# Shift taps of a long-convolution layer as four 32-row tiles of TensorE in place of two 64-row tiles

## The chip, the cores and the metric

The kernel runs on one core of one Trainium2 chip. The metric is the device time of one execution in microseconds; lower is better. Five engines matter here: TensorE (PE, with its weight loads PEld), VectorE (DVE), ScalarE (ACT), GpSimd (POOL), and SyncE (SP), which issues nearly all transfers to the core's 16 DMA engines.

## The reference

There are two kinds of layer, used in turn: A, B, A, B, on 2048 tokens of 512 channels in bf16. The kernel computes the first pass of A once and reuses its product in the second, because that product depends on `k`, `v` and the filters alone.

```
k_shift = sum over t in 0..3 of k_pad[t : t+2048] * shift_k[:, 3-t]   # causal taps, per channel
kv      = k_shift * v
y       = irfft(rfft(kv, 4096) * rfft(ssm_k, 4096))[:2048] + kv * ssm_D
A(x)    = layernorm(x) * y                                    # q = layernorm(x)
B(x)    = gelu(layernorm(layernorm(x)) @ w1 + b1) @ w2 + b2   # 512 -> 1376 -> 512
x = q;  x += A(layernorm(x));  x += B(...);  x += A(...);  x += B(...)
```

(The second layernorm of a normalized value is part of the reference; what matters for this case is only the part that makes `k_shift * v`.)

## The kernel before, in words

**Two halves.** The first half, to about 100 us, makes the convolution `y` by a Fourier transform that is factored into matmuls. The second half is gating, layernorms and the two matmuls of B, nearly all of it on PE.

**The tiles of the first half.** The 512 channels go in four chunks of 128 (`cc` or `ct`, 0 to 3). The filter (`K`) and the product (`U`) each pass a first stage of matmuls (`S0` to `S3`, L327), are evicted from PSUM (`e`, L334 and L336), are turned (`T0`, `T1`: for `K` by PE at L383, for `U` by transposing DMAs at L456), and pass a second stage with the table `Wt` (`K2..` at L393, `X..` at L486). The spectrum of the filter is also needed with neighbouring partitions exchanged: that is done by copies from SBUF to SBUF, two for each of the pieces `sw00`, `sw01`, `sw11` and `sw10` (L403). Spectra are multiplied on DVE (`T00` to `T33`, L495), go back through PE (`V..`, L504), are evicted (L511, L513), turned by transposing DMAs (`TP..`, L549) and multiplied by a last table (`Y..`, L561 and L570).

**The shift taps.** `k` is brought in turned by four transposing loads (`lk0` to `lk3`, L347): `kT` holds channels on the partitions and tokens along the row. For each chunk, the piece `kv0` to `kv3` (L434) computes the causal taps as matmuls: the weights are 128 tokens of `kT` with a stride of 16, and what streams is a table `DG` of diagonal blocks that holds the tap coefficients. A diagonal block needs only its own rows of the array, so the array is divided into `RT` tiles of `RW = 128 // RT` rows that work side by side, each into its own PSUM bank at a time. With `RT = 2` there are 22 passes of two tiles, with up to 256 columns each. `DG` is made by GpSimd (`dg`, L410) from the coefficients `sT` and from an identity folded to `RW` columns (`IDr`, L293). The two products with `v` are `kvm{cc}1` and `kvm{cc}0` on DVE (L448). They read PSUM and write `uv` in place, and then the first stage `U{cc}S0` and so on can start.

**Memory.** Most data lie in one large SBUF tile, `arena`, at offsets written by hand. Those that matter here: `ZK`, the filter's spectrum, from 0; `KSW`, the target of the swap copies, from 32 KB; `uv` from 64 KB to 80 KB; `kT` from 80 KB. The framework adds semaphore waits where it takes two accesses to `arena` to touch each other.

**The order.** Nothing is scheduled at run time. A string `ORDER` names every piece, with the engine that runs it and the PSUM or buffer slot that it takes. The pieces are recorded in this order and each engine runs its own in order. Around `kv3` and `sw00` it reads:

```
kv3.P01 U1T0.S3 K3T0e.D pb0.G K2S3.P2 kvm31.D K3T1.P3 K2S3e.A sw00.S
kvm30.D K3T1e.A K2T0.P2 U1T1.S pc00.D U3S0.P0 U3S3.P1 K2T0e.D
```

Letters: P is PE, D is DVE, A is ACT, S is SP (a transfer), G is GpSimd. `pa`, `pb` and `pc` are the statistics, scale and application of a layernorm; `lx` loads the rest of the residual.

Of the kernel before, what the change touches and what calls it, by code (L numbers as in the profile page):

```python
# [135 lines left out]
def kernel(ctx: ExitStack, tc: tile.TileContext, A_q, A_k, A_v, A_shift_k, A_ssm_k, A_ssm_D,  # L136
# [17 lines left out]
    KDMA = ()  # L154
    UPE = ()
    TPE = (3,)
    RT = 2
    RW = P // RT

    def apf(t, offset, dims):  # L160
# [64 lines left out]
    def view(t, dims, dtype=None):  # L225
        n = int(np.prod(dims))
        v = t[:, :] if dtype is None else t[:, :].bitcast(dtype)
        names = "abc"[:len(dims)]
        return v[:, 0:n].rearrange("p (%s) -> p %s" % (" ".join(names), " ".join(names)),
                                   **dict(zip(names[1:], dims[1:])))  # L230
# [59 lines left out]
    nc.gpsimd.memset(kT[:, :, 17 - KS:16], 0.0)  # L290
    if RT == 4:
        nc.gpsimd.tensor_tensor(IDh[:], IDt[:, 0:64], IDt[:, 64:P], ALU.add)
    nc.gpsimd.tensor_tensor(IDr[:], *((t[:, RW * i:RW * i + RW] for t in (IDh if RT == 4 else IDt[:, :],) for i in (0, 1))),  # L293
                            ALU.add)
# [118 lines left out]
    for cc in range(4):  # L413
# [3 lines left out]
        def taps(it, cc=cc):  # L417
            tiles = [pf[it["slot"]["ps"]], pf[it["slot"]["ps+"]]]
            seen = set()
            for tau in [0] + list(range(1 - KS, 0)) + list(range(1, NT)):  # L420
                for r in range(RT):
                    rows = slice(RW * r, RW * r + RW)
                    first, end = max(tau, 0), min(tau + KS, NT)
                    while first < end:
                        if RT == 2:
                            last = min(end, first // 8 * 8 + 8)
# [12 lines left out]
        for h in range(2):  # L439
            def mul(it, pe=pe, cc=cc, h=h):  # L440
                c0 = cc * CW + 64 * h
                t = pf[pe["slot"]["ps+" if h else "ps"]]
                if RT == 2:
                    us, k = uv[:, :, c0:c0 + 64], view(t, [NT, 64])
# [279 lines left out]
```

## Time and profile before

| | us |
|---|---|
| median of 3 runs | 260.72 (260.39 to 260.88) |
| the profiled execution: time / span of its trace | 260.88 / 259.2 |
| PE busy in the span | 236.0 (91%) |
| PE weight loads | 144.2 (56%) |
| DVE busy | 172.0 (66%) |
| ACT busy | 145.5 (56%) |
| DMA issued by SP (q1), share of 16 engines | 54.2% |

The span is what the trace covers; the time also has what lies around it. In the page's table of 40 slices each digit stands for about 6.5 us of the span and gives the busy share in tenths. In a list of instructions in order of time, the first number is the start in us from the span's start, the second the duration, and a bracket at the end gives the idle time of that engine just before, and what ended it. SPq is the SP queue: its durations are those of issuing a transfer, not of the transfer. A share of busy DMA engines can be over 1, since transfers that overlap on an engine are added.

### The profile page before, as it was taken

Reading aid. Unit: us, or ns where it says so; the run is one execution under the profiler, and the core shown is the slowest. Engines: PE = TensorE matmul, PEld = TensorE weight load, DVE = VectorE, ACT = ScalarE, POOL = GpSimd, SP = SyncE. Lnnn points to the kernel's source line nnn. Section 1 sums busy time; section 2 is a strip of 40 time slices with the busy share of each in tenths; the row PEclk is TensorE's granted clock in tenths of the full one; section 3 lists DMA queues with packets and bytes.
Section 4 is the critical chain, followed back from the end, with each engine's and each line's share of the span. In section 5 each row is a group of like instructions: output and inputs, shape, how many; then the busy total and the mean of one; then the engine's idle time right before and its main releaser. Section 6 shows DMA issues by size and latency. Waiting matters only on the chain.

```text
span 259.2 us, 4520 instructions
## 1 busy us (share of the span) xinstructions
PE 236.0 (91%) x1800; PEld 144.2 (56%) x1800; DVE 172.0 (66%) x347; ACT 145.5 (56%) x199; POOL 28.3 (11%) x54
## 2 busy tenths in 40 slices
PE   7399999969976668999999999999999999999994
PEld 6378888858976535954444444444444444444441
DVE  0558999998898999989987457567677900120232
ACT  2235798788988827895829238268234285055000
POOL 4210000100000321132201101101101100000000
PEclk9979999999999959999999999999999999999999
DMA  6999999999999999920322120050040140010111
GB/s 251 165 280 271 189 340 271 207 282 310 245 303 179 166 226 344 178 42 0 72 40 53 30 52 4 0 82 0 3 81 0 60 104 0 0 72 9 43 70 52
DMA packets 61961, 32.87 MB, mean 127 GB/s; under 512 B 56722, under 2 KB 58868, under 8 KB 60788
## 3 DMA queue, kind: packets, MB, share of 16 engines
q1 hardware_dynamic: 61186, 32.51, 54.2%
q8 instruction: 14, 0.23, 0.4%
q10 hardware_dynamic: 674, 0.07, 0.3%
q0 software_dynamic: 80, 0.00, 0.2%
q14 instruction: 7, 0.06, 0.1%
HBM read 12.40 MB, written 2.10 MB: 56 GB/s over the span
## 4 chain that ended last, share of the span: by engine, by line
PE 69%; DMA 12%; DVE 8%; ACT 6%; issue 2%; SPq 1%; POOL 0%; ACTq 0%; DVEq 0%; POOLq 0%
PE p_89 L680 10%; PE p_92 L680 8%; PE p_91 L658 8%; PE p_92 L658 8%; PE p_89 L658 7%; PE p_90 L658 7%; PE p_90 L680 6%; PE p_91 L680 5%; DMA arena<-in_A_k_dram 4%; DMA ZT_78<-ZT_76 3%; DMA arena<-arena 2%; ACT arena L315 2%; DMA ZT_82<-ZT_81 2%; DVE arena L317 2%; DVE arena L448 2%
## 5 line engine op out<-in xcount | busy, mean ns | idle before, releaser
L658 PEld LDWEIGHTS <-arena 128*128 128x128 bf16 (+1 forms) x396 | 39.6, 100 | 37.9 <-issue 1.3
L680 PEld LDWEIGHTS <-arena 128*128 128x128 bf16 (+1 forms) x352 | 34.4, 98 | 41.7
L680 PE MATMUL p_89<-arena 128*128 128x512 bf16 (+1 forms) x121 | 27.1, 379 | 0.0
L669 ACT ACTIVATE arena<-p_91,B_71 128x512 bf16<-128x512 f32 (+3 forms) x26 | 15.8, 663 | 18.5 <-PE p_92 L680 9.8
L688 DVE TENSOR_TENSOR arena<-p_89,arena 128x1024 bf16<-128x1024 f32 (+1 forms) x4 | 4.4, 1092 | 31.5 <-PE p_89 L680 31.5
L658 PE MATMUL p_91<-arena 128*128 128x512 bf16 (+3 forms) x104 | 23.3, 367 | 0.0
L658 PE MATMUL p_92<-arena 128*128 128x512 bf16 (+3 forms) x108 | 22.4, 351 | 0.0
L680 PE MATMUL p_92<-arena 128*128 128x512 bf16 (+1 forms) x99 | 22.2, 379 | 0.0
L669 ACT ACTIVATE arena<-p_92,B_71 128x512 bf16<-128x512 f32 (+3 forms) x27 | 15.5, 632 | 11.8 <-PE p_92 L658 11.7
L658 PE MATMUL p_89<-arena 128*128 128x512 bf16 (+1 forms) x96 | 18.9, 343 | 1.2 <-ACT arena L315 1.2
L669 ACT ACTIVATE arena<-p_89,B_71 128x512 bf16<-128x512 f32 (+1 forms) x24 | 13.2, 613 | 12.0 <-PE p_90 L680 7.8
L658 PE MATMUL p_90<-arena 128*128 128x512 bf16 (+2 forms) x88 | 19.2, 360 | 0.0
L680 PE MATMUL p_90<-arena 128*128 128x512 bf16 (+1 forms) x77 | 17.3, 379 | 0.0
L327 PEld LDWEIGHTS <-arena 128*128 128x128 bf16 x128 | 11.9, 97 | 6.4 <-issue 2.0
L669 ACT ACTIVATE arena<-p_90,B_71 128x512 bf16<-128x512 f32 (+2 forms) x22 | 13.1, 645 | 4.0 <-PE p_90 L658 2.3
L578 DVE TENSOR_TENSOR arena<-arena 128x1024 bf16<-128x1024 bf16 (+2 forms) x17 | 11.2, 656 | 1.9 <-ACT arena L315 1.1
L680 PE MATMUL p_91<-arena 128*128 128x512 bf16 (+1 forms) x55 | 12.4, 379 | 0.0
L688 DVE TENSOR_TENSOR arena<-p_92,arena 128x1024 bf16<-128x1024 f32 (+1 forms) x4 | 4.4, 1091 | 11.8 <-PE p_92 L680 11.8
L315 ACT ACTIVATE arena<-p_92 128x2048 bf16<-128x2048 bf16 (+2 forms) x6 | 7.0, 1166 | 8.6 <-PE p_92 L383 6.1
L434 PEld LDWEIGHTS <-arena 64*128 64x128 bf16 x176 | 8.9, 149 | 3.6 <-DMA arena<-in_A_k_dram 2.9
L257 DVE BATCH_NORM_STATS2 lst_105<-arena 128x6 f32<-128x512 bf16 x16 | 10.3, 684 | 0.6 <-DMA arena<-in_A_q_dram 0.5
L257 DVE BATCH_NORM_STATS2 lst_97<-arena 128x6 f32<-128x512 bf16 x16 | 10.2, 682 | 0.0
(193 smaller groups left out, 420.8 us busy)
## 6 DMA issues: line engine op xcount, KB each, us to landing
arena<-arena SPq DMA_DIRECT2D x8, 512.0 KB, 4.8
arena<-in_A_ssm_k_dram SPq DMA_DIRECT2D x4, 512.0 KB, 5.6
arena<-in_A_v_dram SPq DMA_DIRECT2D x2, 1024.0 KB, 7.3
arena<-tabM SPq DMA_DIRECT2D x1, 2048.0 KB, 13.1
arena<-in_A_q_dram SPq DMA_DIRECT2D x1, 1536.0 KB, 7.6
arena<-in_B_w_dram SPq DMA_DIRECT2D x1, 1376.0 KB, 6.6
arena<-in_B_w_dram SPq DMA_DIRECT2D x1, 1280.0 KB, 9.9
Wt<-tabW SPq DMA_DIRECT2D x1, 1024.0 KB
```

The costliest lines, as they stand in the source:

```text
L257: nc.vector.bn_stats(self.st[:, i, h, :], xg(g, i, i + 1, c0, c9)[:, 0, :])
L315: nc.scalar.activation(d, s, AF.Copy)
L317: nc.vector.tensor_copy(d, s)
L327: nc.tensor.matmul(o[:, i, :], src[:, 4 * q + i, cs], Ft[:], start=True, stop=True)
L434: nc.tensor.matmul(o, w, DG[rows, cc, first - tau:last - tau, :].rearrange("p t c -> p (t c)"), start=bank not in seen, stop=tau == NT - 1 ...
L448: nc.vector.tensor_tensor(us, k, us, ALU.mult)
L578: nc.vector.tensor_tensor(tmpa[:, a:b, c0:c9], ln[:, a:b, c0:c9], ys, ALU.mult)
L658: nc.tensor.matmul(o[0:m, ft - fts[0], :], W1t[:, ct, ft * P:ft * P + m], lnT[n % 3][:, a:b, ct, :], start=ct == 0, stop=ct == CT - 1)
L669: nc.scalar.activation(hT[n % 2][0:m, ft, a * P:b * P], psv(pe, dims)[0:m, ft - fts[0], :], AF.Gelu_apprx_tanh, bias=B1[0:m, ft:ft + 1])
L680: nc.tensor.matmul(o[:, i - a, :], hT[n % 2][0:m, ft, i * P:(i + 1) * P], W2t[0:m, ft, :], start=ft == 0, stop=ft == FT - 1)
L688: nc.vector.tensor_tensor(xs, psv(pe, [2, D])[:, 0:b - a, :], xs, ALU.add)
```

## The change

The row tiles of the taps become four of 32 rows. The table `DG` has half the columns, the folded identity takes one more addition, every tap pass has four matmuls of up to 128 columns, and each of the four tiles has one PSUM bank for itself, so passes no longer have to be cut at a bank's end (19 passes in place of 22). The product with `v` reads PSUM as two tiles of 16 x 32. `ORDER` is the same. All of it hangs on one constant; the branches were there already:

```diff
@@ -154,7 +154,7 @@
     KDMA = ()
     UPE = ()
     TPE = (3,)
-    RT = 2
+    RT = 4
     RW = P // RT
```

The branches that it switches, from the functions `taps` and `mul` and the set-up (the same text in both kernels):

```
if RT == 4:
    nc.gpsimd.tensor_tensor(IDh[:], IDt[:, 0:64], IDt[:, 64:P], ALU.add)
...
if RT == 2:
    last = min(end, first // 8 * 8 + 8)
    o, bank = tiles[r][:, RW * first:RW * last], (r, first // 8)
else:
    last = end
    h = 512 * (r % 2)
    o, bank = tiles[r // 2][:, h + RW * first:h + RW * last], r
...
if RT == 2:
    us, k = uv[:, :, c0:c0 + 64], view(t, [NT, 64])
else:
    us = uv[:, :, c0:c0 + 64].rearrange("p n (r c) -> p r n c", c=RW)
    k = view(t, [2, NT, RW])
```

## The prediction

> **What bounds the kernel now.** I read the page's 40 slices first, then the SP queue, then DVE and PE in order of time. In the slices, after the first, the 16 DMA engines are busy 90% or more until 110 us, and PE and DVE are nearly full beside them:
>
> ```profile
> PE   7399999969976668999999999999999999999994
> DVE  0558999998898999989987457567677900120232
> DMA  6999999999999999920322120050040140010111
> ```
>
> The SP queue shows why compute speed alone does not move this stage. From 1.7 to 72.1 us it issues one transfer after another with no gap worth naming:
>
> ```profile
> 47.91 2.67 SPq L456 DMA_TRANSPOSE ZT_79<-ZT_80  x1
> 50.77 1.17 SPq L403 DMA_DIRECT2D arena<-arena  x2
> 51.99 4.56 SPq L456 DMA_TRANSPOSE ZT_79<-ZT_80  x1
> 56.65 3.57 SPq L403 DMA_DIRECT2D arena<-arena  x4
> ```
>
> The line at 50.77 is `sw00`, the two swap copies. The first is issued at 50.77, the second at 51.37, and the issues listed by window give the second 4.8 us to landing: both are there at 56.2 us.
>
> ```profile
> arena<-arena SPq DMA_DIRECT2D x1, 512.0 KB, 4.8
> ```
>
> DVE in order of time (brackets: idle before, and for what):
>
> ```profile
> 46.58 1.21 DVE L448 TENSOR_TENSOR arena<-p_90,arena 128x1024 bf16<-128x1024 f32 x1
> 47.71 1.22 DVE L448 TENSOR_TENSOR arena<-p_89,arena 128x1024 bf16<-128x1024 f32 x1
> ...
> 52.88 1.23 DVE L317 CAST arena<-p_90 128x1024 bf16<-128x1024 f32 x1 [0.40 <-PE p_90 L393]
> ...
> 60.82 1.23 DVE L317 CAST arena<-p_90 128x1024 bf16<-128x1024 f32 x1 [0.90 <-PE p_90 L393]
> ...
> 64.63 1.23 DVE L495 TENSOR_TENSOR T_87<-xb_84,arena 128x2048 bf16<-128x2048 bf16 x1 [0.32 <-ACT xb_84 L315]
> ...
> 71.83 1.23 DVE L495 TENSOR_TENSOR T_87<-xb_85,arena 128x2048 bf16<-128x2048 bf16 x1 [1.39 <-DMA arena<-arena]
> ...
> 79.20 1.29 DVE L257 BATCH_NORM_STATS2 lst_105<-arena 128x6 f32<-128x512 bf16 x2 [0.47 <-DMA arena<-in_A_q_dram]
> ```
>
> The first two are `kvm31` and `kvm30`. 71.83 is `T20`, which waits for the swap `sw10`: there the transfer stream is the wall. DVE has only 3.0 us of idle time between `kvm30` and `T20` (0.40+0.90+0.32+1.39), and 1.0 us more behind it (0.47 at 79.20, and 0.55 at 83.79, for ACT).
>
> **The change, part by part.**
>
> *The taps on PE.* 44 matmuls and 44 weight loads per `kv` become 76 and 76: 19 passes of four tiles, 13 of them 128 columns wide. The busy time by stretch gives the four `kv` now; the first ran at half clock (last columns: granted clock, DMA share, GB/s):
>
> ```profile
> 12.44:15.92 3.48, 3.47 (x44) 2.94 (x44) 0.53 1.00 387
> 21.33:23.30 1.97, 1.96 (x44) 1.96 (x46) 1.00 1.41 259
> ```
>
> A 256-column pass starts every 0.107 to 0.11 us at full clock, so 128 columns alone need 0.053. Four short passes in the trace (64, 128, 128 and 64 columns, starts 22.23 to 22.46) took 0.23, that is 0.057 each where columns would ask 0.04: about the floor a pass has for its weight loads. So the likely `kv` is 19 x 0.057 to 0.062 = 1.1 to 1.2 us, saving 0.8; `kv0` at half clock, 2048 columns in place of 4096, about 1.8, saving 1.65. If the two loads of those passes ran one after the other (0.028 each), four would make a pass 0.115 and a `kv` 2.2 us: 0.2 lost. If the tiles do not overlap at all, 76 x 0.057 = 4.3 us. I take 1.15: paired matmuls start 0.00 to 0.02 us apart, so the tiles do overlap. The Trainium skill, "TensorE: Matmul & The Clock Gate", section "Wait — 56ns, not 53.3ns?", says that start-to-start never falls below about 25 ns however narrow the matmul. By that rule, as an estimate, a pass of four costs 100 ns, a `kv` 1.9 us, and the saving vanishes; the sum below is the same by either.
>
> *Where that saving goes.* Nowhere. What `kv0` to `kv2` save by 25 us meets transfers whose order and issue do not depend on it, and whatever is left of it ends at `kvm30`, for the reason that comes next.
>
> *A wait that the change adds.* In the built order the two kernels differ, beside the taps and their tiles, in three waits. In the kernel before, `T00` (57.56) is the first DVE instruction to wait for both copies of `sw00`. In the changed kernel `kvm30` waits for both, and `sw00` waits for `kvm31` and the taps' table. `ORDER` records `sw00.S` before `kvm30.D`; the product's access is now four-dimensional (two tiles of 32 channels), and the framework takes it to touch the copy's target, though `uv` lies from 64 KB and that target at 32 to 40 KB. The wait is in the program, so it will be paid. `sw00` cannot be earlier: SP reaches it at 50.77, behind `U1T0`, and its other inputs were ready at 47.8 or before. So `kvm30` starts at 56.2 in place of 47.71: 8.5 us late. Queued behind it on DVE: `pc00`, `K2T0e`, `pc01`, `K2T1e`, `K206e` and all later work. PE waits with it: `U3S0` (48.98) needs its product, and PE keeps its order. ACT waits for `U3S0`. SP goes on through `U1T1`, then waits for `K206e` before `sw01`.
>
> *What is recovered.* From 56.2 DVE has 24.1 us of its old stretch to `T20` less the 3.0 idle, whose transfers are by then done or not yet the last: 5.5 us late at best. Is `sw10` there? Its last input `K211e` (60.82 to 62.04) comes about 9 late with the clock's loss below, at 71.1; at its old 6.5 us (issued 65.2, landed 71.7) `sw10` lands near 77.6, just ahead of DVE.
>
> *PE's clock.* PE idles from about 48.5 to 57.4. After 2.6 us idle (9.85 to 12.45) it came back at half clock and kept it for 3.5 us:
>
> ```profile
> 15.50:16.00 0.50, 0.50 (x9) 0.50 1.12 248
> 16.00:17.00 1.00, 1.00 (x19) 0.96 1.30 299
> ```
>
> Idle gaps of 1.8 us kept the full clock. Nine us is past both, so `U3S0`, `U3S3` and the 16 transposes of `K2T1` cost 0.85+0.85+1.7 = 3.4 us in place of 1.9, and `K2T1e` and `K206e`, for which DVE waits, come 1.3 later than DVE would have been. With none of this, 5.5 at `T20`; with all of it, 6.8. I take 6.7.
>
> *After `T20`.* The 0.47 and 0.55 are waits for transfers and for ACT behind them that DVE, being later, no longer meets: 6.7 - 1.0 = 5.7. From there to 100 us DVE stays the fullest engine, and the second part of the kernel runs on PE alone; nothing gives more back.
>
> *The rest at nothing.* `kvm`: 8 products of 1.22 us; the closest row, an eviction into runs of 8 elements (L336), also takes 1.22. Pool: one 0.32 us add more at 3.3 us, and the table in half-size products, both in its 7.8 us wait for `sT` (to 11.4). If that cover went, `kv0` would slip by 0.3.
>
> The sum: profiled execution 260.88 (span 259.2 and 1.7 around it) + 5.7 = 266.6; this execution is 0.16 above the median, so 266.4. With 4.5 to 6.2 for the two unknowns, 265.2 to 266.9.
>
> **The rivals.**
>
> *More comes back.* The transfers finish early while compute stands still, so the TP turns after 75 us (eleven issues in 17.9 us, where the shorter of them, at 1.3 each, would make 14.3) run unhindered, or the clock holds: 3 to 4.5 late, 263.7 to 265.2.
>
> *Nothing comes back.* `sw01`, `sw11` and `sw10`, now issued only as compute makes them, land after DVE wants them: 8.5, or with the clock 10: 269 to 271. The tiles not overlapping (`kvm31` and with it `sw00` late) ends here too.
>
> *No slower.* Mechanism: the stage is set by the transfer stream, as SP's row says; it has slack, `sw10`'s inputs being ready at 62.0 and SP reaching it at 65.2. If the wait's delay were under about 3 us the wall at 71.8 would hold and the time stay 260.7; and if the profile's own chain were right (42.71 ACT, 44.66 SP, then the transfer), up to 1.0 of the taps' saving would pass: 259.7. Against: the delay is 8.5.
>
> *The change does nothing for PE* (weight loads set the pass): same time as the forecast, since the saving is not in the sum.
>
> **How the numbers follow.** Forecast 0.60; more back 0.22; nothing back 0.12; no slower 0.06, of which 0.04 faster and 0.02 within 0.2% (0.5 us, about what a measurement of this kernel can tell from no change). Range 264.2 to 268.4: it takes in most of "more back" and leaves out nearly all of the two ends, some 2 in 10.
>
> **What would show it.** Right: `kvm30` (second L448 on p_89) with about 8 us idle before it, put down to a DMA of arena or starting just after `sw00` lands near 56; PE empty from 48 to 57 and clock 0.5 for some 3.5 us after; a `kv` of 1.1 to 1.2 us; `T20` near 78.5. Wrong: `kvm30` without a gap, or `sw00` landing before 52; a gap as told, but `T20` moved by less than 4 or more than 9.

## The result, and the profile after

The changed kernel takes 268.40 us (median of 4 runs, 267.75 to 268.64); before, beside it, 260.56 (4 runs, 259.45 to 260.88). The ratio is 1.0305, 95% interval 1.0269 to 1.0341: 7.9 us slower. The forecast was 266.4, range 264.2 to 268.4: the measured time lies at the range's upper end. The direction and the wait are as told, the size is 2.0 too small. The profiled execution took 268.64, its span 266.9.

Ratios leave out executions more than 1.5% above the fastest of their kernel and medians do not, so a ratio is not always the quotient of two medians, and in two experiments below the profiled execution is such a one (264.98 us where the median is 260.94, and 359.82 at a granted clock of 0.655 where the median is 264.84).

The 40 slices (each now 6.7 us) have a hole in slices 8 to 10, where PE, DVE and the DMA engines fall together, and PE's granted clock falls with them:

```profile
PE   6676999449999738899999999999999999999994
DVE  0476799457999999996988745946857910030132
PEclk9798699968999995999999999999999999999999
DMA  7999999962999999980044040040040150011111
```

SP issues the swap copies `sw00` where it did (50.80, before 50.77); the issues listed by window put the two landings at 54.04 and 55.66 us:

```profile
50.80 1.18 SPq L403 DMA_DIRECT2D arena<-arena  x2
```

DVE in order of time (brackets: idle before, and for what). `kvm31` is at 48.41, and `kvm30` starts just after the second landing; `T20` is the line at 78.78, 86.00 is `pa11`, 90.59 is `T31`:

```profile
48.41 1.21 DVE L448 TENSOR_TENSOR arena<-p_90,arena 128x1024 bf16<-128x1024 f32 x1
55.78 1.22 DVE L448 TENSOR_TENSOR arena<-p_89,arena 128x1024 bf16<-128x1024 f32 x1 [6.15 <-DMA arena<-arena]
...
61.18 1.22 DVE L317 COPY arena<-p_92 128x2048 bf16<-128x2048 bf16 x1 [1.76 <-PE p_92 L383]
62.90 1.22 DVE L317 CAST arena<-p_90 128x1024 bf16<-128x1024 f32 x1 [0.50 <-PE p_90 L393]
...
78.78 1.22 DVE L495 TENSOR_TENSOR T_87<-xb_85,arena 128x2048 bf16<-128x2048 bf16 x1
...
86.00 1.29 DVE L257 BATCH_NORM_STATS2 lst_105<-arena 128x6 f32<-128x512 bf16 x2 [0.33 <-DMA arena<-in_A_q_dram]
...
90.59 1.22 DVE L495 TENSOR_TENSOR T_88<-xb_83,arena 128x2048 bf16<-128x2048 bf16 x1 [0.56 <-ACT xb_83 L315]
```

The waits of that stretch (total, times, longest) show PE standing behind `kvm30`:

```profile
PE p_89 L327 <- DVE arena L448: 6.6, 1, 6.6
DVE arena L448 <- DMA arena<-arena: 6.2, 1, 6.2
```

The taps themselves, by stretch (length, then busy us and instructions of PE, PEld, DVE, ACT, POOL; then granted clock, DMA share, GB/s), `kv0` to `kv3`:

```profile
12.34:13.72 1.38, 1.37 (x77) 1.34 (x78) 0.00 (x0) 0.00 (x0) 0.66 (x3) 1.00 1.04 433
20.15:21.55 1.40, 1.39 (x77) 1.28 (x76) 1.21 (x1) 1.40 (x1) 0.00 (x0) 1.00 1.12 182
21.70:25.82 4.12, 1.63 (x77) 1.51 (x78) 2.48 (x3) 0.01 (x1) 0.00 (x0) 0.86 1.11 261
45.90:47.29 1.39, 1.39 (x79) 1.35 (x78) 1.36 (x7) 0.59 (x1) 0.00 (x0) 1.00 1.18 236
```

The four tiles work side by side: 1.39 us for a `kv`, where the stretch of before had 1.97. (That one ended where the next `kv` began. From its first matmul to the first of the next piece, `kv3` takes 1.30 us, before 2.05; the last 0.2 of the 1.39 are its last matmuls running out.) But `kv2` takes 4.12: PE stands still for 2.5 us in it, and the page puts this down to no wait. PE's clock falls behind it, to 0.50 from 25 to 31 us. That was in no forecast.

### The profile page after: what moved, and what is told of

Same layout as the page of the kernel before. It is cut to its first block, busy times and chain, and to the rows that moved or that the text cites. A ratio compares the mean times of both kernels' runs of the same rounds, so it can differ in the third digit from the quotient of the medians.

```text
span 266.9 us, 4777 instructions
## 1 busy us (share of the span) xinstructions
PE 237.5 (89%) x1928; PEld 144.4 (54%) x1928; DVE 172.0 (64%) x347; ACT 145.9 (55%) x199; POOL 27.8 (10%) x55
## 4 chain that ended last, share of the span: by engine, by line
PE 71%; DMA 7%; ACT 6%; DVE 5%; issue 4%; SPq 4%; POOL 1%; DVEq 0%; ACTq 0%; POOLq 0%
PE p_89 L680 10%; PE p_92 L680 8%; PE p_91 L658 8%; PE p_92 L658 8%; PE p_89 L658 7%; PE p_90 L658 6%; PE p_90 L680 6%; PE p_91 L680 4%; DMA ZT_78<-ZT_76 2%; DMA arena<-in_A_v_dram 2%; SPq L347 2%; DMA arena<-arena 2%; DVE arena L317 2%; PE p_91 L327 1%; PE p_90 L327 1%
## 5 line engine op out<-in xcount | busy, mean ns | idle before, releaser
L327 PEld LDWEIGHTS <-arena 128*128 128x128 bf16 x128 | 14.0, 114 | 14.2 <-DVE arena L448 8.6
L578 DVE TENSOR_TENSOR arena<-arena 128x1024 bf16<-128x1024 bf16 (+2 forms) x17 | 11.2, 657 | 2.8 <-ACT arena L315 2.0
L327 PE MATMUL p_89<-Ft,arena 128*128 128x256 bf16 x32 | 6.2, 327 | 6.7 <-DVE arena L448 6.6
L257 DVE BATCH_NORM_STATS2 lst_97<-arena 128x6 f32<-128x512 bf16 x16 | 10.2, 682 | 0.0
L315 ACT ACTIVATE arena<-p_91 128x1024 bf16<-128x1024 f32 (+1 forms) x8 | 8.2, 1027 | 3.5 <-PE p_91 L570 3.5
```

The source lines that it names most:

```text
L257: nc.vector.bn_stats(self.st[:, i, h, :], xg(g, i, i + 1, c0, c9)[:, 0, :])
L315: nc.scalar.activation(d, s, AF.Copy)
L327: nc.tensor.matmul(o[:, i, :], src[:, 4 * q + i, cs], Ft[:], start=True, stop=True)
L578: nc.vector.tensor_tensor(tmpa[:, a:b, c0:c9], ln[:, a:b, c0:c9], ys, ALU.mult)
```

## The experiments

Four questions: is the false wait of `kvm30` the whole loss; what are the taps worth; what is PE's clock worth; and what is the standstill in `kv2`. Each group below was measured on one chip beside the kernel before, whose median was 261.37 in the first group, 260.04 in the second and 261.07 in the third, so kernels of different groups are compared by their ratios to before. A difference of two ratios is uncertain by about 0.5%, or 1.3 us.

| kernel | median us | ratio to before (95%) |
|---|---|---|
| four tiles, product first | 260.94 | 0.9997 (0.9963 to 1.003) |
| two tiles, product in four dimensions | 268.52 | 1.0284 (1.0241 to 1.0328) |
| two tiles, four passes | 260.06 | 0.9920 (0.9882 to 0.9957) |
| before, PE kept busy late | 260.00; again 259.74 | 0.9932 (0.9900 to 0.9965); 0.9955 (0.9920 to 0.9990) |
| after, PE kept busy late | 265.08 | 1.0195 (1.0158 to 1.0233) |
| after, PE kept busy in the wait | 266.24 | 1.0218 (1.0181 to 1.0254) |
| after, both | 264.84 | 1.0126 (1.0064 to 1.0188) |
| four tiles, product first, more warming | 261.15 (one run) | |
| four tiles, product first, PE kept busy late | 258.72; again 259.88 | 0.9952 (0.9923 to 0.9981); 0.9954 (0.9921 to 0.9987) |
| the same, boundary later | 260.60 | 0.9995 (0.9959 to 1.0031) |

### Four tiles without the wait

The changed kernel with two pieces of `ORDER` exchanged:

```diff
-... K2S3e.A sw00.S kvm30.D K3T1e.A ...
+... K2S3e.A kvm30.D sw00.S K3T1e.A ...
```

> The changed kernel (four tiles) with two pieces exchanged in the written order: the product kvm30 is recorded ahead of the swap copies sw00, so that in the built program kvm30 waits for ACT alone and sw00 waits for it. Theory 1 (the false wait of kvm30 for sw00 is the whole loss, the four tiles are worth about nothing): kvm30 starts near 48.5 to 49.5 us, T20 near 71.8, the time 260.1 to 261.2. Rival A (the loss lies in the four tiles themselves, or in the 2.5 us for which PE stood still in kv2): 265 to 268.6, with kvm30 early all the same. Rival B (the taps' time is on the path, as the page's chain of before has it): 258 to 260.

Measured: 260.94, ratio 0.9997. The loss is gone, with all of the four tiles and the standstill in `kv2` (1.7 us here) still in the kernel. In its profiled execution (264.98) all of DVE is 2.9 late from 28 us on and still 2.92 late at `T20`, so the absolute times of the expectation were not met in it; the two products run without a gap. The profile of the same order with more warming (below, 261.15) shows the same, both products in one row:

```profile
48.35 2.35 DVE L448 TENSOR_TENSOR arena<-p,arena 128x1024 bf16<-128x1024 f32 x2
```

### The wait without the four tiles

The kernel before, with only the product's access written in four dimensions:

```diff
 if RT == 2:
-    us, k = uv[:, :, c0:c0 + 64], view(t, [NT, 64])
+    us, k = (x.rearrange("p n (r c) -> p r n c", c=32)
+             for x in (uv[:, :, c0:c0 + 64], view(t, [NT, 64])))
```

> The kernel before (two tiles of 64 rows) with the product's access written in four dimensions, as four tiles would write it; the arithmetic and the order of pieces are the same, and in the built program kvm30 now waits for both sw00 copies. Theory 1: kvm30 starts near 55.8 us, T20 near 78.5, the time 267 to 268.6: the whole loss without any of the four tiles. Rival A (tiles or the stall in kv2 at fault): 260 to 262.

Measured: 268.52, and DVE in order of time:

```profile
48.52 1.22 DVE L448 TENSOR_TENSOR arena<-p,arena 128x1024 bf16<-128x1024 f32 x1
56.40 1.22 DVE L448 TENSOR_TENSOR arena<-p,arena 128x1024 bf16<-128x1024 f32 x1 [6.67 <-DMA arena<-arena]
```

The whole loss, without one four-tile matmul (`kvm30` and `T20`, at 56.40 and 79.71, are 0.6 and 1.2 later than expected, in an execution that was 1.9 late at `kvm31` already). These two runs settle the first question: the way the product's operands are written makes the wait, and the wait makes the loss. The form itself costs nothing (1.22 us either way).

### What the taps are worth

The kernel before with four of its passes left (it leaves the other passes of the tap sum out):

```diff
-for tau in [0] + list(range(1 - KS, 0)) + list(range(1, NT)):
+for tau in range(0, NT, KS):
```

> The kernel before with only the four passes of shift 0, 4, 8 and 12 in every kv: it leaves out the other passes of the tap sum, so the PE time of a kv falls from 1.97 to about 0.4 us. Theory (the transfer stream sets this stage, a shorter kv ends in a wait for a transfer): 260.1 to 261, within 0.3 of before, T20 again at 71.8. Rival (the page's chain: the taps stand on the path): 258 to 259.7, T20 earlier by 1 to 2.6.

Measured: ratio 0.9920, a gain of 1.1 to 3.1 us by the interval, which takes eight of the twelve executions; in medians of all, 1.3. My expectation of 260.1 to 261 was too firm: something does pass. In the profile `T20` starts at 70.09 in place of 71.83, still behind a transfer, and the next transfer takes it back:

```profile
70.09 4.63 DVE L495 TENSOR_TENSOR T<-xb,arena 128x2048 bf16<-128x2048 bf16 x4 [0.25 <-DMA arena<-arena]
...
78.28 1.29 DVE L257 BATCH_NORM_STATS2 lst<-arena 128x6 f32<-128x512 bf16 x2 [1.29 <-DMA arena<-in_A_q_dram]
```

The wait for `lx` grew from 0.47 to 1.29 us, and by the application `gb2` (98.20, before 98.03) nothing was left on DVE. Some 6 us of PE time were removed (`kv1` and `kv2` went from 1.97 to 0.66, `kv0` from 3.48 to 1.08) and at most half came out. The four tiles remove less: 3.48 + 3 x 1.97 - 4 x 1.39 = 3.8, of which the standstill takes 1.7 to 2.5 back. At the same share that is some 0.3 to 0.9 us (an estimate), less than these intervals can tell from nothing.

### What PE's clock is worth

Filler matmuls of 512 columns whose product is never read, placed where PE stands idle. Late ones (19, ahead of `TP03`, `Y03` and `Y11`) in the kernel before and in the changed one, and 29 in the wait of the changed one:

```diff
-... U1T1.S pc00.D U3S0.P0 ...                   # in the wait (changed kernel)
+... U1T1.S pc00.D f1.P1 U3S0.P0 ...
-... TP11.S TP03.P0 ... gs0.D Y03.P3 ... w1.S Y11.P2      # late
+... TP11.S f2.P3 TP03.P0 ... gs0.D f3.P2 Y03.P3 ... w1.S f4.P2 Y11.P2
```

> The kernel before with 19 filler matmuls of 512 columns (their product is never read) in the idle stretches of PE ahead of TP03, Y03 and Y11, 88 to 94 us. In the trace of before PE ran at half clock from 93.8 to about 98 us after those gaps. Theory 2 (the half clock there is paid in full by the second part): PE stays at full clock from 88 to 98 us, the last piece of that stretch comes 1 to 1.9 us earlier, the time 258.8 to 259.7. Rival (the weights' transfer, landing at 99.65, or DVE sets that place): 260.3 to 261; if the filler itself delays Y11: up to 261.5.

> The changed kernel, false wait and all, with the same 19 filler matmuls ahead of TP03, Y03 and Y11 as in the run of the kernel before with PE kept busy. Theory 2 (about 0.9 us of the 7.8 lost are PE's half clock, which lasts longer after the late TP13): PE at full clock from 95 to 106 us, the time 265.3 to 266.7, 6.5 to 7.2 above the busy kernel before. Rival (the late DVE and transfers set the second part, the clock is beside the path): 267.5 to 268.5, the full 7.8 above before.

> The changed kernel with 29 filler matmuls of 512 columns (product never read) ahead of U3S0, in the 6.6 us for which PE stands empty while kvm30 waits. Theory (the half clock after the stall costs the 1.3 us of the prediction's term before T20): PE at full clock from 57 us, K206e near 61.6 in place of 62.90, T20 near 77.5 in place of 78.78, the time 266.9 to 267.4. Rival (sw10's landing sets T20 whatever the clock): T20 between 78.3 and 78.8, the time 267.8 to 268.6.

> The changed kernel with its false wait and with both sets of filler matmuls: 29 in the 6.6 us before U3S0 and 19 ahead of TP03, Y03 and Y11. What is left of the loss is the wait alone, without PE's clock. If the sum of the prediction holds up to T20 (5.5 late with no clock's loss) and nothing is recovered or lost after it, 5.5 above the busy kernel before on the same chip (5.0 to 6.0). If the 1.0 that the prediction took off after T20 is recovered once the clock is held, 4.5 (4.2 to 4.9). If the clock is beside the path, 6.7 or more.

The late filler in the kernel before gains 0.68% (1.8 us), and 0.45% when run again on another chip; the expected gain was 0.9 to 1.9. The same stretch before and with the filler:

```profile
94.00:96.00 2.00, 2.00 (x6) 0.73 (x5) 1.86 (x11) 0.34 (x1) 0.81 (x2) 0.50 0.86 187
```

```profile
94.00:96.00 2.00, 2.00 (x13) 0.85 (x12) 1.93 (x10) 2.00 (x4) 1.37 (x3) 1.00 1.00 365
```

Six matmuls of 512 columns in 2 us at clock 0.50; at 1.00 eight of them and five of 128 columns. PE is 'busy' in both, and only the clock column tells them apart. With the late filler, B's first matmul then waits last for its weights' transfer, 0.26 to 0.75 us in six such profiles, so that transfer is the next limit.

In the changed kernel the same filler brings the ratio from 1.0305 to 1.0195; against the busy kernel before, measured on other chips, this leaves 2.4 to 2.6% (6.3 to 6.9 us) of the 7.9, so by these ratios the late clock has 1.0 to 1.6 of it. That is near the expected 6.5 to 7.2, but uncertain by 1.3: neither the rival (the full 7.8) nor a share of nothing is excluded.

The filler in the wait brings the ratio from 1.0305 to 1.0218, 2.3 us (0.9 to 3.6 by the intervals), where 1.3 was expected; `K206e` is at 61.24 and `T20` at 77.44, as expected (61.6 and 77.5). The clock by stretch, the changed kernel first:

```profile
57.00:58.00 1.00, 0.94 (x5) 0.70 (x6) 1.00 (x4) 0.00 (x0) 0.00 (x0) 0.50 0.45 85
61.00:62.00 1.00, 1.00 (x9) 0.81 (x8) 0.82 (x1) 0.46 (x1) 0.00 (x0) 0.50 0.00 0
62.00:63.00 1.00, 1.00 (x10) 0.86 (x9) 0.50 (x2) 1.00 (x2) 0.00 (x0) 0.89 0.02 8
```

and with the filler, with DVE in order of time below it:

```profile
57.00:58.00 1.00, 0.36 (x4) 0.33 (x5) 1.00 (x3) 0.00 (x0) 0.00 (x0) 1.00 1.14 219
61.00:62.00 1.00, 0.81 (x8) 0.72 (x8) 1.00 (x2) 1.00 (x3) 0.00 (x0) 1.00 0.00 0
```

```profile
56.36 1.22 DVE L448 TENSOR_TENSOR arena<-p,arena 128x1024 bf16<-128x1024 f32 x1 [6.69 <-DMA arena<-arena]
...
61.24 3.48 DVE L317 CAST arena<-p 128x1024 bf16<-128x1024 f32 x3
...
77.44 3.50 DVE L495 TENSOR_TENSOR T<-xb,arena 128x2048 bf16<-128x2048 bf16 x3 [0.25 <-DMA arena<-arena]
```

From `kvm30` to `T20` this is 77.44 - 56.36 = 21.08 us; in the changed kernel 78.78 - 55.78 = 23.00; before 71.83 - 47.71 = 24.12. So in these profiles the half clock behind the wait costs 1.9 us (1.3 were forecast), and without it all of DVE's 3.0 us of old idle time come back: 24.12 - 3.0 = 21.1. (Two more profiles with the wait and nothing in it have 23.31 and 22.37.)

With both fillers the ratio is 1.0126 (four of six executions), 1.7% (4.5 us; 2.6 to 6.3 by the intervals; 5.1 in medians) above the busy kernel before on the same chip. This agrees with 7.9 less 2.3 less 1.0 to 1.6 for the clock, and speaks against the clock being beside the path (6.7 or more); between 5.5 and 4.5 it does not decide.

### The standstill in kv2

In the list of PE's matmuls, counted from the start, the first run without the wait and the changed kernel both stop after the 349th. The experiment adds 16 matmuls at the start:

```diff
-for i in range(28):          # warming matmuls
+for i in range(44):
```

> Four tiles with the product recorded ahead of the swap copies, and 16 more warming matmuls at the start. In both four-tile runs PE stood still for 1.7 to 2.5 us between the 349th and the 350th matmul of the program, the 225th tap. If the cause is the fetching of PE's instructions (a block of the program not there yet), the stall stays between the 349th and the 350th matmul of the program, now the 209th tap, and so 16 taps earlier. If something in the data is waited for, it stays at the 225th tap, the 365th matmul. If it depends on chance, there is none. Time as the kernel before, 260 to 262, plus 0 to 1 for the longer warming.

PE in order of time, first the four-tile kernel with 28 warming matmuls, then with 44:

```profile
25.33 1.36 PE L434 MATMUL p<-arena 32*128 32x128 bf16 x73 [0.17 <-DVE ZT L336]
28.39 0.24 PE L434 MATMUL p<-arena 32*128 32x32 bf16 x3 [1.70 <-issue]
```

```profile
22.87 1.15 PE L434 MATMUL p<-arena 32*128 32x128 bf16 x57 [0.16 <-DVE ZT L336]
26.41 0.60 PE L434 MATMUL p<-arena 32*128 32x128 bf16 x19 [2.39 <-issue]
```

The stop moved from the 73rd to the 57th matmul of `kv2`, 16 earlier, and stayed behind the 349th of the program, so it belongs to the place in the program and not to the data. All eight profiles of four-tile kernels with the boundary inside `kv2` stop there, seven for 1.7 to 2.5 us and one (359.82) for 0.8; none of the two-tile kernels that were looked at does (before passes its 349th matmul at 35.7 us, without a gap). The pages' instruction queue fits this, before (1800 matmuls) and after (1928):

```profile
q8 instruction: 14, 0.23, 0.4%
```

```profile
q8 instruction: 15, 0.25, 0.4%
```

That 128 more matmuls and 128 more weight loads make one packet more, some 16 KB, is an estimate from these two rows. The times of these packets in the traces show the rest. In the changed kernel PE stops at 22.86, a packet of 16 KB moves from 22.91 to 24.10, and PE goes on at 25.55; in all eight profiles PE goes on 1.36 to 1.45 us after the end of such a packet. The packet before it began 6.3 to 6.6 us earlier, and in no trace here do two begin less than 4.8 us apart. At the pace of `kv3` (76 matmuls in 1.30 us) 128 matmuls last 2.2 us: by this estimate four tiles use up a packet faster than the next one comes. So PE waits for its own instructions. The time of one run, 261.15, is as expected.

### Does the standstill swallow the gain?

The four-tile kernel with the wait mended and the late filler, and the same with 14 warming matmuls of 256 columns in place of 28 of 128, so that the boundary falls behind `kv2`; the two busy kernels were run again beside it:

```diff
-for i in range(28):
-    nc.tensor.matmul(pf[3][:, 0:P], IDt[:], IDt[:], start=True, stop=True)
+for i in range(14):
+    nc.tensor.matmul(pf[3][:, 0:2 * P], IDt[:],
+                     IDt[:].unsqueeze(1).to_broadcast([P, 2, P]), start=True, stop=True)
```

> Four tiles, the product recorded ahead of the swap copies, and the 19 filler matmuls: the change without its false wait, on the busy kernel before. Theory (wait is the whole loss, clock worth 1 to 1.8 us): 258.8 to 260, the same as the busy kernel before within 0.5. Rival (the shorter kv passes some of its saving on, now that PE's clock holds): 257.5 to 258.7.

> The busy kernel before once more (two tiles, 19 filler matmuls), as the base for the other three runs on the same chip. Ratio to before 0.990 to 0.9965 if the first measurement holds.

> Four tiles, product ahead of the swap copies, the 19 filler matmuls, and the warming done by 14 matmuls of 256 columns in place of 28 of 128: the 350th matmul of the program then lies 11 matmuls behind the end of kv2 instead of inside it. If the standstill there is what swallows the four tiles' gain: kv2 takes 1.4 us without a gap, kvm20 follows kvm10 without one, the standstill (1.5 to 2.5 us) shows in KT2 behind it, and the time is 0.3 to 1.3 below the same kernel with 28 (rerun beside it). If the transfer stream swallows the gain anyway: within 0.3 of it.

> Four tiles, product ahead of the swap copies, 19 filler matmuls, once more and on the same chip as the busy kernel before. If the four tiles bring nothing by themselves: within 0.5 us of that kernel. If they pass some of the saved 3.9 us of taps on: 0.6 to 1.5 below it.

On one chip the busy kernel has 0.9955 with two tiles and 0.9954 with four, 259.74 and 259.88 us: within the 0.5 expected for four tiles that bring nothing by themselves, even with PE's clock held; the intervals leave room for 1.3 us either way. The first measurement of four tiles (258.72, base 260.04) has the same ratio. With the boundary moved, `kv2` ran without a gap (21.67 to 23.08) and its product `kvm20` started at 24.11, 1.7 earlier than in the kernel before. Then PE stood all the same (PE in order of time, then the stretch):

```profile
24.23 0.60 PE L327 MATMUL p<-Ft,arena 128*128 128x256 bf16 x4 [1.15 <-DVE arena L448]
28.17 1.93 PE L365 MATMUL p<-IDt,arena 128*128 128x128 bf16 x16 [3.34 <-DMA arena<-in_A_ssm_k_dram]
```

```profile
24.20:28.20 4.00, 0.63 (x5) 0.32 (x4) 2.24 (x2) 1.02 (x1) 0.00 (x0) 0.64 1.48 177
```

The line at 28.17 is `KT2`, and it waits for the filter's load `lK2`, which landed at 28.13. In the kernel before that load landed at 25.94 and `KT2` started at 26.35: only 0.4 us of cover. So in that profile the taps' gain ended at this load, with the standstill out of the way. It was an unusual landing, though: of the sixteen that the trace has for this load, fifteen came by 25.46 and one at 28.12, where in the other profiles the last came at most 1.1 us behind the one before it. The ratio, 0.9995, is no better than with the standstill (0.9954), rather worse, and the expected 0.3 to 1.3 us did not come; the difference, 1.1 us, is within the uncertainty of 1.3. PE's clock averaged 0.64 over that stretch. The expectation that the standstill would show in `KT2` failed too: by then PE's instructions were there.

The other profiles answer the question better. With the standstill, PE went on 0.75 to 0.85 us before `lK2` landed in every one of seven (25.55 and 26.30 in the changed kernel), and `KT2` began 0.04 to 0.6 us after the landing; with two tiles it began 0.04 to 1.0 us after it. So a `kv2` that ends earlier finds this load in its way, standstill or none, and little of the standstill itself is paid at `KT2`. What the shorter `kv0`, `kv1` and `kv3` could pass on by other ways is not separated by any run.

## Why the prediction was right or wrong

**The wait: right.** It named the instruction, its cause and its place; `kvm30` came 8.07 us late (8.5 forecast, the copies landing at 55.66 in place of 56.2). The two experiments that undo and that isolate it settle it. Single profiles differ, however: `kvm31`, ahead of the wait, starts between 46.5 and 48.7 us in the profiles with two tiles and between 45.9 and 49.8 in those with four (without that of 359.82), and 1.83 later in the changed kernel's profile than in that of before. PE's pieces ahead of the wait were as late, so PE stood empty for 6.6 us (50.5 to 57.05) and not for nine. Differences of a microsecond between one profile and another are therefore weak, and those within one profile are better.

**Up to `T20`: right in sum, with two terms off against each other, which is luck.** 78.78 measured, 78.5 forecast. The recovery of DVE's 3.0 us of idle time is as told (21.08 against 21.1). The clock's loss was taken as 1.3 and is 1.9: the half clock lasted 5.2 us after the wait, from 57 to about 62.2, not the 3.5 of the row that the forecast used. The earlier landing gave 0.4 of it back. `sw10` landed at 77.63, as forecast (77.6).

**After `T20`: the step that failed.** "Minus 1.0" was taken off for two waits that DVE, being later, would not meet. Both were met again: 0.33 us for 0.47 at `pa11`, 0.56 for 0.55 at `T31`; the two-tile kernel with the same wait has 0.35 and 0.56. What they wait for hangs on DVE itself: SP issues `lx` behind `sw10`, which is issued only when compute has made its input (`lx` at 71.59 became 78.28, +6.7), and `T31` needs an eviction (`X31e`, 82.73 became 89.54, +6.8) whose matmuls stand in PE's order behind `Y00`, which waits for a turn of DVE's products (`TP00`, 75.06 became 82.11, +7.05). The forecast treated both as fixed points in time. DVE's lateness at `T32` was 6.8, so 0.15 came back and not 1.0. With the late filler, which holds PE's clock, the stretch from `T20` to the end of the span took 185.7 us with the wait, and 185.4 and 186.1 in the two profiles without it (four tiles with the product first: 185.6 and 185.7, and 187.8 with the later boundary, where the clock fell at 83 us): nothing came back there. The chain is read from the trace; no run here changes it alone.

Then, in this profile, 0.95 was lost more. PE at the end of the first half, before and after (`Y11`, `Y10`, `Y30`, `Y31`, and the first matmuls of B):

```profile
93.76 1.86 PE L570 MATMUL p_91<-ZT_77,GPt 128*128 128x512 bf16 x4 [1.67 <-DMA ZT_77<-ZT_81]
95.42 1.91 PE L570 MATMUL p_90<-ZT_77,GPt 128*128 128x512 bf16 x4
97.12 1.46 PE L570 MATMUL p_89<-ZT_82,GPt 128*128 128x512 bf16 x4
98.42 1.03 PE L570 MATMUL p_92<-ZT_82,GPt 128*128 128x512 bf16 x4
...
101.53 1.91 PE L658 MATMUL p_89<-arena 128*128 128x256 bf16 x16 [1.19 <-ACT arena L315]
```

```profile
100.77 1.86 PE L570 MATMUL p_91<-ZT_77,GPt 128*128 128x512 bf16 x4 [2.25 <-DMA ZT_77<-ZT_81]
102.43 1.91 PE L570 MATMUL p_90<-ZT_77,GPt 128*128 128x512 bf16 x4
104.14 1.91 PE L570 MATMUL p_89<-ZT_82,GPt 128*128 128x512 bf16 x4
105.84 1.41 PE L570 MATMUL p_92<-ZT_82,GPt 128*128 128x512 bf16 x4
...
109.28 1.91 PE L658 MATMUL p_89<-arena 128*128 128x256 bf16 x16 [1.13 <-ACT arena L315]
```

`Y11` is 7.01 late. Before, the full clock came back in the middle of the third of these pieces (1.46, then 1.03); after, only in the fourth (1.91, then 1.41). B begins 7.75 late, and the end stays there (span +7.7). So the term after `T20` was -1.0 in the forecast and +0.8 in the trace; with 0.25 at `T20`, less 0.1 by which medians and profiled executions differ, this is the 2.0 that were missed. "Nothing gives more back" was right; that something could take more was left out, although the half clock at 92 to 98 us stood in the profile of before.

The -1.0 failed in every profile with the wait (`T20` to `T31` takes 11.3 to 12.0 us in four of them, 11.2 to 12.0 in three without); the +0.8 is less firm, and its cause stays partly open. The two-tile kernel with the same wait loses about as much in all (268.52), but its PE had the clock back sooner, in the second half of this row:

```profile
101.84 4.89 PE L570 MATMUL p<-ZT,GPt 128*128 128x512 bf16 x16 [1.66 <-DMA ZT<-ZT]
108.87 1.36 PE L658 MATMUL p<-arena 128*128 128x256 bf16 x11 [1.24 <-ACT arena L315]
```

From `Y11` to B this is 7.03 us, where before has 7.77 and the changed kernel 8.51; with the late filler it is 5.8 to 6.2, wait or none. In the traces' records of the clock the half clock is one stretch of 6.8 us in each of the three, and ends 4.2 us after `Y11` began before, 5.8 in the changed kernel and 2.6 here. So these differences follow where that stretch happens to lie. Whether the changed kernel loses more to it than the kernel before on average (1.0 to 1.6 by the ratios above, uncertain by 1.3) is not settled.

**The taps.** A `kv` was to take 1.15 us and takes 1.39 with the last matmuls' running out; its passes start about 0.064 apart (1.16 from the first start to the last), near the forecast 0.057 to 0.062, and `kv3` keeps PE 0.75 shorter, where 0.8 was forecast. `kv0` ran at full clock, not at the half clock forecast. The whole lies between that estimate and the 1.9 us that the rule of the Trainium skill would make ("TensorE: Matmul & The Clock Gate", section "Wait — 56ns, not 53.3ns?", start-to-start never below about 25 ns). With four tiles side by side 76 matmuls took 1.38 us, 18 ns each, and the four of a pass of `kv0` start within some 15 ns, so the measurement stands against that rule for tiles of this kind. As the forecast said, the time of the kernel does not depend on which is right. That the saving goes "nowhere" was too strong: the kernel with four passes gained 1.1 to 3.1 us. For the four tiles alone it holds within the intervals.

**The rivals.** "No slower" had the right stage but is refuted by the two runs on the wait. "More comes back" failed in both its conditions: the clock did not hold (0.50 to 62.2 us), and the transposing turns took no less time (`TP00` 7.05 late, `Y11`, which waits for one of the last, 7.01). "Nothing comes back" was nearer to the time than to the mechanism: 1.1 us did come back before `T20` (24.12 became 23.00).

**A version below both.** The kernel before with 19 idle matmuls ahead of `Y11`, and equally the four tiles with the product first and the same filler, run at 0.993 to 0.9955 of before, each measured twice: 1.2 to 1.8 us less.

## What to carry to other kernels

When a view gains a dimension in a tile that many transfers share, read the waits of the built program before the cost of the instruction: here the instruction's time did not change, and the wait it gained was worth 3%. A later engine recovers an idle gap only if what ended that gap does not itself hang on the engine: follow each releaser back before a wait is taken off the sum. And ask of every new idle stretch on PE what the clock does behind it, and behind the gaps that were there before.

## What was not expected of the hardware

- A place in the program at which PE stands still for 1.7 to 2.5 us with no wait for data, always behind the 349th matmul, in a stretch where it runs through matmuls of 18 ns and 16 DMA engines are full. That it is the fetching of instructions is shown by its place in the program and by the packets of the instruction queue, 1.36 to 1.45 us after whose end PE goes on; that the full DMA engines are what makes it so long was not tried.
- The half clock after an idle stretch lasted 5.2 us (57 to 62.2) and, at the end of the first half, over 6 us (about 100 to 106.7; before 92 to 98), where the first such stretch of the profile before had shown 3.5. In the clock records of these traces a half-clock stretch, but for the one that the end cuts off, is 3.4, 6.8 or, once, 10.2 us long. A standstill of 1.70 us in `kv2` kept the full clock (two profiles), one of 2.19 us or more lost it (five); before `Y11`, two gaps close together (1.83 and 0.78 us in the profile before, with half clock from 91.2) lost it too.
- Matmuls whose product nobody reads make a kernel 0.5 to 0.7% faster, by holding the clock for those that follow.
